# Attention and GEGLU block on one core: TensorE no longer waits for its own semaphore

## The chip, the cores and the metric

The kernel runs on one core of a Trainium2 chip. The metric is the device time of one execution in microseconds (us); before the change it is 1253.1 us, the median of 3 runs (1252.99 to 1253.51). Lower is better.

## What is computed

One transformer block on x of 2048 tokens x 512 features in bf16: a layer norm, attention with 32 heads of 16 features, a residual, a second layer norm, a GEGLU feed-forward of 1792 hidden features, a residual.

```python
qkv = (layernorm(x) @ wqkv) -> q, k, v          # 32 heads, Dh = 16
p = softmax(q @ k^T * Dh**-0.5)                 # 2048 x 2048 for each head
h = x + (p @ v) @ wo
out = h + (gelu(layernorm(h) @ w_gate) * (layernorm(h) @ w_up)) @ w_down
```

## The kernel before

**Units and ticks.** The queries are cut into 8 groups of 256 tokens, the heads into 8 slots of 4. A unit is one slot of one group: 64 units, 8 to a group. A unit has 16 ticks, and a group 128. In a tick two things happen to two units that lie 24 ticks apart:

- pass 1 (`p1_pair`, L797): two matmuls of 32 rows x 512 columns write scores into a pair of banks, and one VectorE reduce (`p1_consume`, L806) takes their row maxima. From tick 20 on the pairs are banks 0-1 and 2-3 in turn, so the pair of tick t is free again when the reduce of tick t-2 is done. 1024 ticks make 1024 reduces. At the end of a unit GpSimd joins the maxima, and a DMA transpose (L846) brings them back into the queries.
- pass 2 (`p2_tile`, L867): four matmuls of 32 rows x 256 columns write two banks, called tile a and tile b here, and two ScalarE exponentials (L879) take them to SBUF. These banks come from a pool of four, 4 to 7, one of which is lent to the dense stream at a time.

**The dense stream.** Behind pass 1 and pass 2 of a tick, TensorE gets one piece of a list of work items: the projections (L676, L739) early on; `item_pv`, probabilities times values (L893); `item_ofin` (L919); the output projection `item_oproj` (L998); `gate_up_mms` (L1072); `down_mm` (L1122). Where a tick has no piece, two dummy matmuls of 128 x 512 (L1285) stand there. An item of PV belongs to one unit and is cut into four pieces, each in a tick of its own. A piece is two halves of 8 matmuls (4 heads side by side in the array's columns, two key tiles one after the other), all 8 pieces of a unit's halves adding up in one bank. A feed-forward item and a projection item are cut into two pieces, a `down` item into pieces of three matmuls. The group's pieces go to TensorE in the order of the Python calls; all engines' orders are fixed when the program is built.

**Waits.** `Plan` keeps, for each tile and bank, its last writer and its readers since. `op` (L96) collects them as dependencies, `_waits_for` (L72) drops those that the engine is already known to have seen, and the rest become waits on the semaphores of the engines. A matmul with `sig=True` raises TensorE's semaphore when it completes; one with `sig=False` is given the token of the next one that signals (L107). A dependency on the own engine is dropped at L75 where its signal has not been issued yet (`v > e.count`), and where a wait for a reader implies it; otherwise TensorE waits for its own semaphore.

In PV the last matmul of each half signals (`sig=(g == 3 and i == 1)`, L893-895), and the first of the next half writes the same bank. In `gate_up_mms`, the projections and `down_mm` the earlier pieces do not signal, so their token is that of the next signal on TensorE: the second pass 1 matmul of the next tick. `group_begin` and `group_end` gather the waits of pass 1 and tile a at the first matmul of the tick.

Of the waits before the change, 580 instructions of TensorE wait for its own semaphore: 386 in PV (L893), 95 in gate and up (L1072), 57 in down (L1122), 27 in the projections (L676, L739), 14 in the output projection (L998), 1 in the warm-up (L427). In 569 of them it is the only wait and sits on the weight load of the matmul.

Of the kernel before, what the change touches and what calls it, by code (L numbers as in the profile page):

```python
# [15 lines left out]
class Plan:  # L16
# [55 lines left out]
    def _waits_for(self, e, deps, extra=()):  # L72
        need = {}
        for (k, v) in list(deps) + list(extra):
            if k == e.name and v > e.count:  # L75
                continue
            if v > need.get(k, 0):
                need[k] = v
        need = {k: v for k, v in need.items() if e.known.get(k, 0) < v}
        waits = []  # L80
        for k, v in sorted(need.items(), key=lambda kv: kv[0] == e.name):
            implied = {}
            for k2, v2 in need.items():
                if k2 != k and (k2, v2) not in self.dropped:
                    self._learn(implied, k2, v2)
            if implied.get(k, 0) >= v and self.behind.get((k, v)) is not None:
                self.dropped.add((k, v))
                continue
            waits.append((k, v))
        self.dropped.clear()  # L90
        for k, v in waits:
            self._learn(e.known, k, v)
        self.n_waits += len(waits)
        return waits
# [1312 lines left out]
```

## Time and profile before

| | |
|---|---|
| median of 3 runs | 1253.1 us |
| profiled execution, its own time | 1253.52 us |
| its span in the profile | 1251.8 us |
| TensorE matmul busy (PE) | 93 % |
| VectorE busy (DVE) | 95 % |
| ScalarE busy (ACT) | 96 % |
| GpSimd busy (POOL) | 61 % |

The span is the stretch that the profile shows; the execution's own time is 1.7 us longer. A "busy" share is the share of the span covered by instructions. Instructions that follow each other on an engine overlap: 23 reduces in a row, whose mean length is 1219 ns, take 26.03 us, 1.131 us each. PEld is TensorE's weight load, which runs beside its matmuls. A row of the timeline gives start, length, engine, line, operation, tiles and how many were merged, and in brackets how long the engine had been idle and what ended that.

### The profile page before, as it was taken

Reading aid. Unit: us, or ns where it says so; the run is one execution under the profiler, and the core shown is the slowest. Engines: PE = TensorE matmul, PEld = TensorE weight load, DVE = VectorE, ACT = ScalarE, POOL = GpSimd, SP = SyncE. Lnnn points to the kernel's source line nnn. Section 1 sums busy time; section 2 is a strip of 40 time slices with the busy share of each in tenths; the row PEclk is TensorE's granted clock in tenths of the full one; section 3 lists DMA queues with packets and bytes.
Section 4 is the critical chain, followed back from the end, with each engine's and each line's share of the span. In section 5 each row is a group of like instructions: output and inputs, shape, how many; then the busy total and the mean of one; then the engine's idle time right before and its main releaser. Section 6 shows DMA issues by size and latency. Waiting matters only on the chain.

```text
span 1251.8 us, 31448 instructions
## 1 busy us (share of the span) xinstructions
PE 1165.3 (93%) x12680; PEld 405.5 (32%) x12680; DVE 1193.7 (95%) x1088; ACT 1200.7 (96%) x2464; POOL 764.0 (61%) x1540
## 2 busy tenths in 40 slices
PE   8999998899999999999999999999999999999998
PEld 3222222233323333233323333233332333233335
DVE  8999999999999999999999999999999999999923
ACT  7899999999999999999999999999999999999992
POOL 7557774467746765376645776367654766547760
PEclk9999999999999999999999999999999999999989
DMA  4101004300010000200010000100001000100000
GB/s 150 31 21 28 24 19 129 88 6 3 6 31 12 6 6 6 38 5 6 4 26 18 3 6 6 26 17 6 6 4 39 6 4 6 26 19 3 6 13 18
DMA packets 50801, 27.45 MB, mean 22 GB/s; under 512 B 36065, under 2 KB 49633, under 8 KB 50657
## 3 DMA queue, kind: packets, MB, share of 16 engines
q1 hardware_dynamic: 50656, 25.45, 7.9%
q8 instruction: 101, 1.65, 0.5%
q14 instruction: 44, 0.35, 0.1%
HBM read 11.80 MB, written 2.10 MB: 11 GB/s over the span
## 4 chain that ended last, share of the span: by engine, by line
ACT 41%; PE 28%; DVE 27%; POOL 2%; issue 2%; DMA 0%; POOLq 0%
DVE PM L806 27%; ACT PTM L879 23%; ACT PTG L879 7%; PE pbank L893 7%; PE pbank L797 5%; PE pbank L867 4%; ACT PTE L879 4%; PE pbank L1122 4%; PE pbank L1285 3%; ACT th_sb L1055 2%; ACT g_sb L641 1%; PE pbank L1072 1%; PE pbank L739 1%; PE pbank L998 1%; ACT OA L641 1%
## 5 line engine op out<-in xcount | busy, mean ns | idle before, releaser
L806 DVE TENSOR_REDUCE PM<-pbank 128x2 f32<-128x1024 f32 x1024 | 1166.3, 1219 | 11.4 <-PE pbank L867 5.0
L879 ACT ACTIVATE PTM<-pbank 128x512 bf16<-128x512 f32 x1388 | 740.2, 672 | 11.2 <-PE pbank L867 4.5
L867 PE MATMUL pbank<-QT,KT 32*128 32x256 bf16 x4096 | 487.6, 273 | 5.4 <-ACT PTM L879 1.9
L797 PE MATMUL pbank<-KT,QT 32*128 32x512 bf16 x2048 | 394.1, 384 | 17.8 <-DVE PM L806 6.5
L1285 PE MATMUL pbank<-ones_bf,ident 128*128 128x512 bf16 x794 | 245.8, 385 | 23.6 <-ACT PTM L879 2.8
L879 ACT ACTIVATE PTG<-pbank 128x512 bf16<-128x512 f32 x420 | 228.4, 663 | 2.1 <-PE pbank L867 1.6
L797 PEld LDWEIGHTS pbank<-KT,QT 32*128 32x128 bf16 x2048 | 100.0, 91 | 356.2 <-DVE PM L806 164.7
L867 PEld LDWEIGHTS pbank<-QT,KT 32*128 32x128 bf16 x4096 | 159.5, 92 | 56.1 <-ACT PTM L879 30.5
L893 PE MATMUL pbank<-PTM,VA 128*17 128x256 bf16 x2776 | 154.8, 275 | 15.5 <-ACT PTM L879 0.6
L879 ACT ACTIVATE PTE<-pbank 128x512 bf16<-128x512 f32 x240 | 138.4, 672 | 2.6 <-PE pbank L867 1.5
L832 POOL TENSOR_TENSOR MX<-PM,MX 128x8 f32<-128x8 f32 x64 | 12.9, 202 | 162.9 <-DVE PM L806 162.9
L928 POOL TENSOR_TENSOR LINV<-OAT,negone 128x16 f32<-128x16 f32 (+1 forms) x32 | 92.7, 2896 | 0.0
L1285 PEld LDWEIGHTS pbank<-ones_bf,ident 128*128 128x128 bf16 x794 | 47.6, 97 | 126.0 <-ACT PTM L879 80.3
L893 PEld LDWEIGHTS pbank<-PTM,VA 128*17 128x17 bf16 x2776 | 42.7, 87 | 108.0 <-PE pbank L893 74.3
L821 POOL TENSOR_TENSOR MX<-PM,MX 128x8 f32<-128x8 f32 x64 | 13.0, 203 | 103.7 <-DVE PM L806 103.3
L1072 PE MATMUL pbank<-hnT_l,wu_sb 128*128 128x256 bf16 x448 | 66.7, 275 | 3.4 <-ACT PTM L879 0.2
L1072 PE MATMUL pbank<-hnT_l,wg_sb 128*128 128x256 bf16 x448 | 66.9, 275 | 2.5
L1114 POOL TENSOR_TENSOR GUT<-th_sb,u_sb 128x512 bf16<-128x512 f32 x49 | 62.3, 1271 | 4.5 <-DVE u_sb L630 2.4
L1061 POOL TENSOR_TENSOR th_sb<-th_sb,g_sb 128x512 f32<-128x512 f32 x49 | 62.1, 1268 | 4.1
L1062 POOL TENSOR_TENSOR th_sb<-g_sb 128x512 f32<-128x512 f32 x49 | 51.0, 1041 | 21.8 <-ACT g_sb L641 21.8
L1064 POOL TENSOR_TENSOR th_sb<-th_sb,g_sb 128x512 f32<-128x512 f32 x49 | 62.1, 1267 | 3.1
L1122 PE MATMUL pbank<-wd_sb,GUT 128*128 128x512 bf16 x224 | 60.7, 382 | 3.2 <-ACT PTM L879 0.2
(149 smaller groups left out, 1085.1 us busy)
## 6 DMA issues: line engine op xcount, KB each, us to landing
QKS<-QKS SPq DMA_DIRECT2D x27, 112.0 KB, 2.2
x_sb<-in_A_x_dram SPq DMA_DIRECT2D x4, 512.0 KB, 5.5
xres<-in_A_x_dram SPq DMA_DIRECT2D x16, 128.0 KB, 2.2
out_dram<-out_sb SPq DMA_DIRECT2D x16, 128.0 KB, 1.7
wg_sb<-in_B_w_gate_dram SPq DMA_DIRECT2D x4, 448.0 KB, 4.5
wu_sb<-in_B_w_up_dram SPq DMA_DIRECT2D x4, 448.0 KB, 4.0
wd_sb<-in_B_w_down_dram SPq DMA_DIRECT2D x3, 512.0 KB, 6.7
STG<-ST SPq DMA_TRANSPOSE x64, 2.3
```

What stands on the lines that cost most here:

```text
L797: P.op("pe", lambda e, g=g, b=b: e.matmul(pbank[:, b, :], QT[32 * g:32 * g + 32, c, slot, 128 * qt:128 * qt + 128], KT[32 * g:32 * g + 32, ...
L806: P.op("dve", lambda e: e.tensor_reduce(out=PM[:, par, qt, kc, g:g + 2], in_=pbank[:, b:b + 2, :], axis=AX.X, op=ALU.max), reads=[("pb", b ...
L867: P.op("pe", lambda e, kt=kt, i=i: e.matmul(pbank[:, b, 256 * i:256 * i + 256], KT[32 * g:32 * g + 32, slot, 128 * kt:128 * kt + 128], QT[ ...
L879: P.op("act", lambda e, b=b, pi=pi: e.activation(out=PTt(pi), in_=pbank[:, b, :], func=ACT.Exp), reads=[("pb", b)], writes=[("PT", pi)], e ...
L893: P.op("pe", lambda e, g=g, kt=kt, pi=pi, i=i: e.matmul(pbank[32 * g:32 * g + 17, b, 0:256], VA[:, kt, 4 * slot + g, :], PTt(pi)[:, 256 * ...
L928: P.op("pool", lambda e: e.tensor_tensor(out=li, in0=oat4[:, :, :, 16], in1=negone[:, 0:8 * ns].rearrange("p (q h) -> p q h", q=2), op=ALU ...
L1061: o(1.27, lambda e: e.tensor_tensor(out=ts_, in0=ts_, in1=gs, op=ALU.mult), [("th", par), ("g", par)])], then=done)
L1064: o(1.27, lambda e: e.tensor_tensor(out=ts_, in0=ts_, in1=gs, op=ALU.mult), [("th", par), ("g", par)])], then=lambda: defer(TANH_LAG, lamb ...
L1072: P.op("pe", lambda e, dc=dc, fc=fc, i=i: e.matmul(pbank[:, b, 256 * i:256 * i + 256], w[:, dc, 128 * fc:128 * fc + 128], hT[:, dc, :], st ...
L1114: P.op("pool", lambda e: e.tensor_tensor(out=o_ap, in0=shp(ts_), in1=shp(us), op=ALU.mult), reads=[("th", par), ("u", par)], writes=o_keys ...
L1122: P.op("pe", lambda e: e.matmul(pbank[:, b, :], GUT[:, fc, 128 * k:128 * k + 128], wd_sb[:, fc, :], start=first, stop=last), reads=[("GUT" ...
L1285: P.op("pe", lambda e: e.matmul(pbank[:, b, :], ident[:], ones_bf[:, 0:512], start=True, stop=True), reads=["ident", "ones_bf"], writes=[( ...
```

## The change

In `_waits_for` every dependency of TensorE on its own semaphore is dropped, not only the ones not yet signalled.

```diff
     def _waits_for(self, e, deps, extra=()):
         need = {}
         for (k, v) in list(deps) + list(extra):
-            if k == e.name and v > e.count:
+            if k == e.name and (v > e.count or k == "pe"):
                 continue
             if v > need.get(k, 0):
                 need[k] = v
```

All 580 waits go; 11 of these instructions keep waits for other engines. The order of the instructions on the five engines, the banks, the tiles, the signals and the waits of all other engines are the same.

## Prediction

> **What bounds the kernel now.** I read the page's engine rows first, then the waits, then the timeline tick by tick, and last the chain. DVE, ACT and PE are all over 90% busy, so the share of busy time does not name the bound.
>
> ```profile
> PE 1165.3 (93%) x12680; PEld 405.5 (32%) x12680; DVE 1193.7 (95%) x1088; ACT 1200.7 (96%) x2464; POOL 764.0 (61%) x1540
> ...
> ACT 41%; PE 28%; DVE 27%; POOL 2%; issue 2%; DMA 0%; POOLq 0%
> ...
> L806 DVE TENSOR_REDUCE PM<-pbank 128x2 f32<-128x1024 f32 x1024 | 1166.3, 1219 | 11.4 <-PE pbank L867 5.0
> ```
>
> The starts of the 1024 reduces decide it: 867 of the 1023 distances between them are 1.13 us, what a reduce needs when nothing holds it up. DVE is thus the pace of the whole middle, and only a tick that is late against 1.131 us costs time. Lateness over the whole span is 22.1 us: 5.7 in ticks 0 to 23, where the projections fill TensorE and, going by the order of waits, hardly any own wait stands, and **16.3 us after that**, in some 80 ticks. These 16.3 us and the end behind the last reduce are all that this change can touch. The waits of TensorE by releaser:
>
> ```profile
> PEld pbank L893 <- PE pbank L893: 104.7, 314, 0.4
> ...
> PEld pbank L1072 <- PE pbank L867: 13.4, 62, 0.3
> PEld pbank L1122 <- PE pbank L867: 12.4, 42, 0.3
> ```
>
> The first row is the second half of a PV piece waiting for the first. The reader is to see that 104.7 us of waiting is no gain of 104.7 us: most of it lies in ticks where DVE is not done either. A tick where it counts, from the timeline:
>
> ```profile
> 705.73 0.11 PEld L867 LDWEIGHTS pbank<-QT,KT 32*128 32x128 bf16 x2 [0.58 <-ACT PTE L879]
> ...
> 706.05 0.11 PEld L893 LDWEIGHTS pbank<-PTM,VA 128*17 128x17 bf16 x8 [0.21 <-issue]
> ...
> 706.52 0.11 PEld L893 LDWEIGHTS pbank<-PTM,VA 128*17 128x17 bf16 x8 [0.36 <-PE pbank L893]
> ...
> 706.85 0.39 PE L797 MATMUL pbank<-KT,QT 32*128 32x512 bf16 x2
> ...
> 707.28 3.49 DVE L806 TENSOR_REDUCE PM<-pbank 128x2 f32<-128x1024 f32 x3 [0.42 <-PE pbank L867]
> ```
>
> ACT let go of tile b's bank 0.7 us late (705.73). PV followed 0.32 us later, its second half 0.47 after the first, the next pass 1 0.33 after that, and the reduce 0.43 after pass 1: DVE stood idle for 0.42 us.
>
> **What each wait is worth on PE.** *PV, second halves: 256 of the 386.* From the first half's start to the second's is 0.469 us in every piece of the trace. A half is two rounds of 256 columns. Without the wait they should follow at the pitch of matmuls that wait for nothing: the chain has 48 matmuls of 256 columns in 5.24 us (L1072 in the tail), 0.109 each, so 0.22 for two. Saving 0.25 a piece. The bounds: 0.25, and nothing, if the array holds back a matmul that adds onto a region still being drained; within a half the second round already adds onto the first 0.11 us later, so I take 0.25. A PV tick falls from 0.33 + 0.47 + 0.33 = 1.13 us of PE, exactly DVE's pace, with no way to catch up, to 0.88. *PV, first halves: 130.* Their signal is a tick old: nothing. *down, 42 pieces.* Their first matmul starts 0.453 after pass 1, because the signal waited for is pass 1's own; the dummies, which wait for no such thing, start 0.332 after it (600.78 to 601.11). Saving 0.12: the tick falls from 1.206 to 1.086. *gate, up and projections, 122.* Also 0.45 against 0.33, but these ticks need only 0.99 us (0.45 + 0.54), and in the median the late tile b holds them until 0.65 anyway: nothing. *oproj, 14, and the warm-up's one*: hidden in the same way.
>
> **What of it reaches the end.** From about 300 us on the late ticks repeat in every group of 128 ticks (146.9 us). I follow each from the release before it that PE does not move.
>
> - *PV behind a late bank.* In the tick above ACT runs without a gap from 690.56 to 706.2, and it began when a tanh waited for GpSimd, which waited for a DMA and a reduce at 680.7. So 705.73 stays, and pass 1 comes 0.25 earlier. Six ticks of 0.51 late: 6 x 0.25 = 1.5. Ten more of 0.33 to 0.35: 10 x 0.25 = 2.5.
> - *PV ticks that were less than 0.25 late, or followed another PV*: seven of 0.20, five of 0.14, six of 0.05 and six single ones of 0.11 to 0.17 (62 to 83, 227 and 263 to 265 us) go to nothing: 1.4 + 0.7 + 0.3 + 0.8 = 3.2.
> - *down.* Six groups have four ticks that are 0.18, 0.08, 0.08 and 0.24 late. The 0.08 are the tick of 1.206. But ACT runs without a gap around them and gives tile b's bank 0.3 late in the first and the last, so the lateness mostly moves to the last. ACT itself begins its busy stretch some 0.24 earlier, since the PV ticks ahead of it (idle ACT 0.33 + 0.16 + 0.05) are shorter. Of 0.58 I take 0.24 as gone: 6 x 0.24 = 1.4, and 0.2 for ticks of 0.03 after the other down item.
> - *Not touched*: 1.2 us of late ticks with dummies behind a late bank (0.20 x 6), the projection ticks at 53 to 61 us, what is left above.
> - *Behind the last reduce* ACT is the pace until 1220.3; it idles ahead of exponentials at 1200.6, 1202.8 and 1218.8 for 0.12, 0.27 and 0.09 behind PV, and two PV halves after the last exponential save about 0.4: 0.9.
>
> The sum is 4.0 + 3.2 + 1.6 + 0.9 = **9.7 us**. Against the profiled execution's own 1253.52 that is 1243.8; that run was 0.4 above the median, so I predict **1243.4**.
>
> **The rivals.**
>
> *A, ACT, GpSimd and the DMA transposes decide, or the matmuls serialise anyway.* Then PV ticks keep their length, or the late banks move with them. For: ACT holds 41% of the chain, and the late ticks begin with an ACT release. Against: the reduce's idle time ends with PE, 0.43 after a pass 1 that PV held back, and ACT's distances between exponentials at their shortest, 0.478, leave it some 5% free. It would give 1251 to 1253.5.
>
> *B, nearly all lateness goes.* With PE at 0.88 in PV ticks ACT is fed earlier in every unit and its stretches start sooner, so the late banks go too. 16.3 + 0.9 would give 1236. Against: the tanh's wait on GpSimd starts ACT's stretch at 690.56 whatever PE does.
>
> *C, slower: the clock.* The granted clock was halved twice:
>
> ```profile
> 22.90:26.30 3.40, 3.40 (x12) 0.86 (x11) 2.87 (x4) 2.44 (x4) 3.21 (x6) 0.50 0.00 0
> 600.00:603.40 3.40, 3.35 (x32) 1.11 (x29) 3.40 (x4) 3.40 (x9) 0.54 (x4) 1.00 0.00 0
> ...
> 1207.35:1214.18 6.83, 6.32 (x28) 1.69 (x28) 0.30 (x1) 5.83 (x13) 6.58 (x7) 0.50 0.00 1
> ```
>
> The columns are the window, its length, busy time of PE, PEld, DVE, ACT and POOL, the clock, DMA share and GB/s. If idle PE drops the clock, PV ticks will do it now, since 0.25 of 1.13 us becomes idle. At half speed a PV tick's array time of 0.21 + 4 x 0.107 = 0.64 doubles, and with the 0.23 of switches the tick is 1.5, 0.37 more than DVE's pace; a drop of 3.4 us, the shortest seen, loses 0.37 x 2.3 = 0.85. Twelve drops eat the gain, fifteen make it slower by over 0.2%; one in each of 64 units would give 1243.4 + 54 = 1298. Against: a tick with dummies holds the same 0.64 of array time (0.21 + 2 x 0.21) and needs 0.87 of PE, and in the second row above, three such ticks, the clock stayed at 1.00. The Trainium skill speaks for this rival ("TensorE: Matmul & The Clock Gate", A second HAM failure mode: psum-queue depth-cycling): there, short idle times between groups of matmuls, in a kernel that cycles through PSUM banks, made the clock swing between half and full. The dummy ticks of this trace, which cycle through banks in the same way, do not show it.
>
> **How the numbers follow.** The forecast, 6 to 14 us faster, 0.72; B, 0.08; a smaller gain of 2.5 to 6 us, between the forecast and A, 0.08; A, 0.07; C, 0.05. A measurement of this kernel can tell about 0.2% (2.5 us) from no change. The smaller gain counts as faster, so faster is 0.88, same 0.07, slower 0.05. The range runs from just under B's 1236, 1235.5, to 1249.5, which cuts off half of the smaller gains, A and C: 0.16 left out.
>
> **What would show it.** The second half's weight load should start without the 0.36 of idle time, 0.22 after the first, and the row of 104.7 us should be gone, replaced by pass 1 waiting for DVE. Ticks of 0.20 and 0.14 late should be gone, those of 0.51 should be near 0.25 and those of 0.33 near 0.08. Wrong: second halves still at 0.47 (A); late ticks of 0.51 gone altogether (B); a clock under 1.00 between 30 and 1200 us (C).

## The result and the profile after

1243.37 us, the median of 4 runs (1242.92 to 1243.8), against 1253.17 us before: the ratio is 0.992, 95% interval 0.990 to 0.994. The change made the kernel 9.8 us faster. The profiled execution took 1243.15 us.

The page of the kernel after, the rows that answer to those of before:

```profile
PE 1137.8 (92%) x12680; PEld 437.8 (35%) x12680; DVE 1189.8 (96%) x1088; ACT 1199.9 (97%) x2464; POOL 764.3 (62%) x1540
...
DVE 58%; ACT 30%; PE 9%; POOL 2%; issue 1%; DMA 0%
...
L806 DVE TENSOR_REDUCE PM<-pbank 128x2 f32<-128x1024 f32 x1024 | 1162.4, 1224 | 5.3 <-PE pbank L867 2.8
```

TensorE's part of the chain that ended last fell from 28% to 9%, VectorE's rose from 27% to 58%: the reduce now sets more than half of it, ScalarE 30%. Of the reduce's idle time, 11.4 us, 5.3 are left. In the waits after, the row of 104.7 us (PV behind PV) is gone, and pass 1 waits for VectorE more often. The first row is from before, the two others from after:

```profile
PE pbank L797 <- DVE PM L806: 6.5, 35, 0.3
```

```profile
PEld pbank L893 <- issue: 40.3, 191, 0.2
...
PE pbank L797 <- DVE PM L806: 23.6, 103, 0.3
```

Where the time went, from the starts of the 1024 reduces in both traces:

| stretch of the span | before, us | after, us |
|---|---|---|
| up to the first reduce | 14.7 | 14.7 |
| lateness against 1.131 us a tick, ticks 0 to 23 | 5.7 | 4.7 |
| lateness, ticks 24 to 1022 | 16.4 | 7.3 |
| behind the start of the last reduce | 58.0 | 57.7 |

9.0 us are the change's work in the middle. The 0.3 at the end are no more than profiles differ there: that stretch is 57.7 and 57.6 us in two profiles of the kernel after, and 57.2 to 58.9 in those of the experiments. The 1.0 us at the start is not its doing: the clock was halved at 22.9 us in the profiled execution before, and not in the one after; of the profiles of the experiments below, with and without the waits, some have that drop and are 5.7 us late there, the others 4.7.

The tick shown before, in the kernel after (timeline, same group and tick):

```profile
699.83 0.11 PEld L867 LDWEIGHTS pbank<-QT,KT 32*128 32x128 bf16 x2 [0.64 <-ACT PTE L879]
...
700.15 0.33 PEld L893 LDWEIGHTS pbank<-PTM,VA 128*17 128x17 bf16 x16 [0.21 <-issue]
700.15 0.61 PE L893 MATMUL pbank<-PTM,VA 128*17 128x256 bf16 x16
...
700.70 0.39 PE L797 MATMUL pbank<-KT,QT 32*128 32x512 bf16 x2
```

The 16 weight loads of a piece are now one row: no idle time parts the halves. From PV's first matmul to the next pass 1 it is 0.55 us instead of 0.80; between the first matmuls of the halves 0.223 instead of 0.469 (their weight loads run ahead, 0.118 apart). And the tick is only 0.03 us late, not 0.51.

Late ticks by their place in a group of 128 (six groups, medians; five groups for tick 22):

| tick | what is behind pass 1 and 2 | late before, us | late after, us |
|---|---|---|---|
| 22 | PV | 0.14 | none |
| 48, 49, 50, 51 | down | 0.18, 0.08, 0.08, 0.24 | 0.17, none, none, 0.38 |
| 54 | PV | 0.05 | none |
| 56 | dummies | 0.20 | 0.26 |
| 86 | PV | 0.51 | 0.03 |
| 89 | PV | 0.33 | 0.08 |
| 119 | PV | 0.20 | none |

### The profile page after: what moved, and what is told of

The parts are those of the page before. It is cut to its first block, busy times and chain, and to the rows that moved or that the text cites. A ratio compares the mean times of both kernels' runs of the same rounds, so it can differ in the third digit from the quotient of the medians.

```text
span 1241.4 us, 31438 instructions
## 1 busy us (share of the span) xinstructions
PE 1137.8 (92%) x12680; PEld 437.8 (35%) x12680; DVE 1189.8 (96%) x1088; ACT 1199.9 (97%) x2464; POOL 764.3 (62%) x1540
## 4 chain that ended last, share of the span: by engine, by line
DVE 58%; ACT 30%; PE 9%; POOL 2%; issue 1%; DMA 0%
DVE PM L806 57%; ACT PTM L879 17%; ACT PTG L879 5%; ACT PTE L879 3%; PE pbank L1122 2%; PE pbank L867 2%; PE pbank L797 1%; ACT th_sb L1055 1%; PE pbank L1072 1%; ACT g_sb L641 1%; ACT OnT L1012 1%; ACT u_sb L641 1%; PE pbank L739 1%; PE pbank L998 1%; PE pbank L676 1%
## 5 line engine op out<-in xcount | busy, mean ns | idle before, releaser
L867 PE MATMUL pbank<-QT,KT 32*128 32x256 bf16 x4096 | 498.2, 273 | 9.7 <-ACT PTM L879 4.4
L797 PEld LDWEIGHTS pbank<-KT,QT 32*128 32x128 bf16 x2048 | 104.5, 91 | 392.7 <-DVE PM L806 170.3
L867 PEld LDWEIGHTS pbank<-QT,KT 32*128 32x128 bf16 x4096 | 164.5, 92 | 65.7 <-ACT PTM L879 36.8
L893 PE MATMUL pbank<-PTM,VA 128*17 128x256 bf16 x2776 | 125.8, 274 | 2.7 <-ACT PTM L879 1.2
L893 PEld LDWEIGHTS pbank<-PTM,VA 128*17 128x17 bf16 x2776 | 60.1, 89 | 46.9 <-issue 29.1
L1072 PE MATMUL pbank<-hnT_l,wu_sb 128*128 128x256 bf16 x448 | 67.1, 276 | 3.1 <-ACT PTM L879 0.2
L1072 PE MATMUL pbank<-hnT_l,wg_sb 128*128 128x256 bf16 x448 | 66.9, 275 | 2.5
```

The costliest lines, as they stand in the source:

```text
L797: P.op("pe", lambda e, g=g, b=b: e.matmul(pbank[:, b, :], QT[32 * g:32 * g + 32, c, slot, 128 * qt:128 * qt + 128], KT[32 * g:32 * g + 32, ...
L867: P.op("pe", lambda e, kt=kt, i=i: e.matmul(pbank[:, b, 256 * i:256 * i + 256], KT[32 * g:32 * g + 32, slot, 128 * kt:128 * kt + 128], QT[ ...
L893: P.op("pe", lambda e, g=g, kt=kt, pi=pi, i=i: e.matmul(pbank[32 * g:32 * g + 17, b, 0:256], VA[:, kt, 4 * slot + g, :], PTt(pi)[:, 256 * ...
L1072: P.op("pe", lambda e, dc=dc, fc=fc, i=i: e.matmul(pbank[:, b, 256 * i:256 * i + 256], w[:, dc, 128 * fc:128 * fc + 128], hT[:, dc, :], st ...
```

## The experiments

**Theory.** The 256 waits of the second halves of PV cost all of it. Without them TensorE has a lead over VectorE again after each late bank, and ScalarE gets its scores earlier. **Rivals:** each of the 580 waits costs something, met or not; the down ticks carry a good part; what is left late is TensorE's or a DMA's.

### The waits of second halves alone, and all others alone

`own` is a new argument of `op`; where it is false, a dependency of TensorE on itself is dropped.

```diff
-writes=[("pb", b)], sig=(g == 3 and i == 1))
+writes=[("pb", b)], sig=(g == 3 and i == 1), own=(m % 2 == 0))
```

> Own waits dropped at the 256 second halves of the PV pieces alone; the other 324 (130 first halves, 95 gate and up, 57 down, 27 projections, 14 output projection, 1 warm-up) stay. Theory (only the second halves stand between a late bank and pass 1): 1243.4 to 1244.2 us, nearly all of the gain; down ticks again 0.075 late in the middle of their four, the four together about as late as without the waits (0.55 to 0.58). Rival (each own wait costs something, met or not): 256 of 580 waits give 256/580 of 9.8 us, 1248.8 us.

Measured: 1244.13 us (1243.64 to 1245.84, 5 runs), ratio 0.993 (0.992 to 0.995). The theory held, the rival of 1248.8 did not. Lateness after tick 24 is 9.0 us; ticks 49 and 50 are 0.076 late again and tick 51 is 0.24; with tick 48's 0.15 that is 0.54 us. In three of the six groups of the profiled run tick 74 is 0.12 to 0.32 late and tick 86 0.26; in the other three neither is late. In just these three groups the DMA transpose of the maxima was late at the same place: from GpSimd's last step before it to the use of its result 4.28, 4.37 and 4.46 us, against 3.76 in the others, and GpSimd idled behind it for 0.47 to 0.66.

In the counterpart only the second halves wait:

```diff
-extra_deps=(), own=True):
+extra_deps=(), own=False):
...
+writes=[("pb", b)], sig=(g == 3 and i == 1), own=(m % 2 == 1))
```

> The other part alone: the 256 waits of the second halves stay, the other 324 are dropped. Theory: 1252.5 to 1253.2 us, late ticks of 0.51, 0.33 and 0.20 as before. Rival (each own wait costs something): 1247.7 us. If down ticks were worth what the prediction gave them (1.6 us): 1251.5 us.

Measured: 1251.72 us (1251.12 to 1252.18), ratio 0.999 (0.998 to 1.000). That is a gain of 1.2 us, under the theory's 1252.5, and far from 1247.7. By its time alone it could be the 1251.5 that the down ticks would give; the ticks say otherwise. The ticks of 0.51, 0.33 and 0.20 stand at 0.50, 0.33 and 0.20. In the four down ticks the two of 0.08 are gone and the last is 0.38 instead of 0.24: the time moved, as 0.149 + 0.378 = 0.53 shows. What is gained is small change: 0.02 to 0.04 in ticks 22, 34 and 48 of each group, some 0.55 us in all, one tick of 0.17, and 0.4 behind the last reduce, which is within the differences there.

### Odd units and even units

Nearly all the late PV ticks belong to odd units. The kernel for the even units has `ui % 2 == 1` in this place.

```diff
-sig=(g == 3 and i == 1))
+sig=(g == 3 and i == 1), own=(m % 2 == 0 or ui % 2 == 0))
```

> Own waits dropped at the 128 second halves of PV pieces of odd units (those that run in the ticks that were late), the rest as before. If a late bank's release stays where it is and PV behind it only shortens (the prediction's step): ticks of 0.51 become 0.25, those of 0.33 become 0.08, of 0.20 and 0.14 go; 7 to 8 us gained, 1245.2 to 1246.2 us. Theory from the profile after (PV of even units feeds ScalarE earlier, so the release itself moves by 0.23 as well): the same here, since even units keep their waits, but then 0.03 instead of 0.25 needs both.

Measured: 1247.24 us (1246.77 to 1248.44), ratio 0.996 (0.995 to 0.997). The tick in question, in the timeline:

```profile
703.18 0.11 PEld L867 LDWEIGHTS pbank<-QT,KT 32*128 32x128 bf16 x2 [0.83 <-ACT PTE L879]
703.50 0.33 PEld L893 LDWEIGHTS pbank<-PTM,VA 128*17 128x17 bf16 x16 [0.21 <-issue]
704.05 0.39 PE L797 MATMUL pbank<-KT,QT 32*128 32x512 bf16 x2
...
704.48 1.23 DVE L806 TENSOR_REDUCE PM<-pbank 128x2 f32<-128x1024 f32 x1 [0.17 <-PE pbank L867]
```

PV behind the bank is as short as in the kernel after, and the tick is 0.25 late in all six groups, just what the prediction gave it. Tick 89 is 0.08 late, tick 119 0.11 and not gone, and a tick of 0.06 is new in each group. That makes 1 us less than expected.

> Own waits dropped at the 128 second halves of PV pieces of even units, in which hardly a tick was late. If the release of a late bank stays (the prediction's step): almost nothing, 1252.3 to 1253 us, ticks of 0.51 unchanged. Theory (TensorE's lead over VectorE grows in these ticks, ScalarE is fed earlier and begins its stretch without a gap earlier): six ticks of 0.51 become about 0.28, 1.4 us, and with two early ticks and the end 1251.0 to 1251.6 us.

Measured: 1250.57 us (1249.93 to 1251.63), ratio 0.998 (0.997 to 0.999), 0.4 us under what the theory gave.

```profile
703.63 0.11 PEld L867 LDWEIGHTS pbank<-QT,KT 32*128 32x128 bf16 x2 [0.58 <-ACT PTE L879]
703.95 0.11 PEld L893 LDWEIGHTS pbank<-PTM,VA 128*17 128x17 bf16 x8 [0.21 <-issue]
704.41 0.11 PEld L893 LDWEIGHTS pbank<-PTM,VA 128*17 128x17 bf16 x8 [0.36 <-PE pbank L893]
704.75 0.39 PE L797 MATMUL pbank<-KT,QT 32*128 32x512 bf16 x2
...
705.17 1.23 DVE L806 TENSOR_REDUCE PM<-pbank 128x2 f32<-128x1024 f32 x1 [0.37 <-PE pbank L867]
```

PV behind the bank is as long as before, with its 0.36 of idle time, and still the tick is 0.27 late instead of 0.51 (five of six groups; 0.45 in the other, where the transpose of the maxima took 4.09 us instead of 3.76). So the bank itself came 0.24 earlier against VectorE: PV of the even unit one block of 16 ticks ahead had let ScalarE start earlier. The two halves of the cause add up: 0.25 + 0.24 of 0.51. Tick 119 falls from 0.20 to 0.11 in the one run and 0.12 in the other, and goes with both.

### The clock: fewer dummies

The second kernel of the two has 1 in the place of 0.

```diff
             if p1_ok:
-                want = 2
+                want = 0 if p2_started else 2
```

> The changed kernel without the dummy matmuls from tick 24 to the last tick of pass 1 (426 of 794 rows of them fewer; the output is not concerned). It tests rival C of the prediction, that idle time on TensorE halves its clock. If it does: the clock falls under 1.00 between 30 and 1200 us; a tick with a PV piece at half speed needs about 1.5 us, each drop of 3.4 us costs up to 0.85 us, dozens of drops give 1255 to 1300 us. If it does not: the clock stays at 1.00, the ticks of 0.26 with a dummy behind a late bank shorten, 1241.5 to 1243.4 us.

Measured: 1311.39 us (1302.43 to 1321.3), ratio 1.047 (1.043 to 1.051). The row of the granted clock in 40 slices, and two stretches of it (window, its length, busy time of PE, PEld, DVE, ACT, POOL, clock, DMA share, GB/s):

```profile
PEclk9997777687898776877888877788889878787879
```

```profile
423.40:440.40 17.00, 15.76 (x152) 5.92 (x152) 14.82 (x14) 15.30 (x32) 9.99 (x20) 0.50 0.01 1
440.60:454.00 13.40, 9.75 (x150) 4.43 (x146) 13.33 (x13) 13.19 (x28) 11.71 (x17) 1.00 0.03 6
```

At 1.00 the reduces run without a gap (13.33 of 13.40 us), and TensorE is busy for 9.75; at 0.50 TensorE is busy for 15.76 of 17.00 us, and VectorE waits. Between 30 and 1190 us the clock was halved for 406 us in all, and lateness after tick 24 rose from 7.3 to 74.2 us. The commonest lateness is 0.38 (78 ticks), as the prediction's 0.37. The rival that the prediction called C is a real mechanism; the kernel after did not meet it in either of its two profiles.

> The changed kernel with one dummy matmul instead of two in each of those ticks, half the idle time of the run without dummies. If the clock falls below some share of busy time: between the changed kernel and the run without dummies, with fewer drops, or none. If it does not fall at all: 1242 to 1243.6 us.

Measured: 1248.25 us (1246.06 to 1250.43), ratio 0.996 (0.995 to 0.998), some 5 us slower than the kernel after. In its profile the clock was halved six times between 30 and 1190 us, for 3.4 or 6.8 us; tick 56 is 0.04 late instead of 0.26, so the dummies themselves do cost there. TensorE's busy share goes with the drops: 92% in the kernel after (no drop between 30 and 1190 us), 87% here, 84% without dummies.

### What is still late: ScalarE

Square of the second layer norm on 64 columns instead of 512, so that 7/8 of each sum of squares is left out:

```diff
-e.activation(out=hn_sb[:, k, :], in_=hh, func=ACT.Square, ...)
+e.activation(out=hn_sb[:, k, 0:64], in_=hh[:, 0:64], func=ACT.Square, ...)
```

> The changed kernel with ScalarE's Square of the second layer norm (L1012, 512 columns, twice a group) cut to its first 64 columns, so that the variance is wrong: it leaves out 7/8 of that work, some 0.37 us each. Theory (what is left of the late ticks, 0.38 and 0.26 in each of six groups, is ScalarE's overload around the output projection): both shrink by about the time taken away, to under 0.1, 1239.5 to 1241 us. Rival (they come from TensorE's down pieces or from DMA): unchanged, 1243 to 1243.8 us.

Measured: 1240.17 us (1238.86 to 1240.32), ratio 0.990 (0.989 to 0.991). Groups by line, shapes, count, busy time, mean ns; in the kernel after and here:

```profile
L1012 ACT ACTIVATE OnT<-xres 128x512 bf16<-128x512 bf16 x14 | 9.8, 697 | 0.0
```

```profile
L1012 ACT ACTIVATE OnT<-xres 128x64 bf16<-128x64 bf16 x14 | 4.4, 314 | 0.0
```

0.38 us less of ScalarE, twice a group, and the ticks of 0.38 (51) and 0.26 (56) are gone in all six groups; tick 48, ahead of the Squares, keeps 0.14. TensorE's down pieces were not touched. (Two groups of this run have a late transpose, 4.34 and 4.44 us, and again ticks 74 and 86 late, the latter by 0.26.) What ticks 51 and 56 lose is ScalarE's burst.

The same work, later:

```diff
-            defer(2, sq)
+            defer(14, sq)
```

> The changed kernel with the two Squares of a group issued about ten ticks later (defer of 14 ticks instead of 2), after ScalarE's stretch without a gap; nothing is left out. If lateness is ScalarE's burst there: 0.38 and 0.26 shrink or go, 1239.5 to 1242 us, unless the later feed-forward puts its own bursts where there is no slack. If ScalarE's load only moves with it: 1243 to 1245 us.

Measured: 1242.06 us (1241.85 to 1245.32), ratio 0.992 (0.991 to 0.993), the same as the kernel after within the interval. Ticks 51 and 56 are no longer late, but tick 84 is 0.33, 90 0.09 and 121 0.08: the burst moved. In the profiled run one tick was 1.0 late: TensorE stood idle for 1.31 us ahead of a gate matmul (L1072 at 833.15), and the clock fell for 3.4 us behind it.

### Attempts to go on

```diff
-                want = 2
+                want = 0 if p2_started and tick % 128 == 56 else 2
```

> The changed kernel without the two dummy matmuls of one tick in each group, tick 56 of 128, the one that is 0.26 late with dummies behind a late bank. If what is left there is the dummies' own time behind ScalarE's release: 0.26 becomes 0.04 as with one dummy everywhere, six times 0.22, 1241.9 to 1242.6 us, and the clock stays at 1.00, since one tick in 128 is no idle window. If ScalarE alone sets it: unchanged, 1243 to 1243.8 us.

Measured: 1242.54 us (1241.6 to 1243.53), ratio 0.992 (0.991 to 0.993). Tick 56 is no longer late, the clock stays at 1.00 between 30 and 1190 us, and the median is 1.2 us under that of the kernel after on the same chip (below), with intervals that overlap.

> The version with the two Squares of a group issued later, without the dummies of tick 84 of 128, which is 0.33 late there. Expected: 0.33 goes, six times 0.3, 1240 to 1241 us, the fastest so far. If the lateness moves to the next PV ticks: 1241.5 to 1242.2 us.

The edit is that of the later Squares with the dummies left out at tick 84. Measured: 1248.84 us (1245.98 to 1252.08), ratio 0.997 (0.996 to 0.998): a miss. Lateness moved to ticks 85 and 86 (0.19 + 0.17), and the clock fell. In the profile the first drop of the middle follows a stretch in which TensorE had half of its time idle:

```profile
831.70:835.10 3.40, 1.70 (x20) 0.82 (x20) 2.59 (x4) 1.90 (x5) 0.65 (x4) 1.00 0.05 6
835.10:838.50 3.40, 3.40 (x24) 1.24 (x21) 3.00 (x3) 3.11 (x7) 1.94 (x4) 0.50 0.00 0
```

TensorE stood there for the first gate matmul of the group, whose input is transposed by a DMA (L988) issued at 829.9 us; the matmul started at 833.9. With the Squares later this transpose is just in time, and in that group it was not; the profile of the later Squares alone has the same gap there. The second drop, of 3.4 us at 992.1, has another place: it follows a tick 84, whose reduce starts at 990.4 and whose dummies are left out, and in the 3.4 us ahead of it TensorE was never idle for more than 0.23 us at a time. The clock also speaks for the dummies: its mean is 0.989 to 0.995 over the six runs here, and 0.996 to 1.000 over the five of the later Squares alone (on another chip), from which this kernel differs only by the dummies of tick 84. So most likely leaving them out lowered the clock, which leaving out those of tick 56 did not. Why the one tick can do without them and the other cannot is open.

The kernel after once more, on the chip of the two runs above:

> The changed kernel as it is, on the same chip as the two others. 1243.0 to 1243.8 us. In its profile, like in those before: lateness of 9 us less after tick 24 than in the kernel before, and the first 24 ticks 4.7 or 5.7 us late according to whether the clock was halved at 23 us, which is the same for both kernels.

Measured: 1243.76 us (1243.53 to 1244.04), ratio 0.993 (0.992 to 0.994): 9.0 us faster than the kernel before on that chip (1252.78). Lateness after tick 24 is 7.2 us, and 4.7 in the first 24 ticks.

## Why the prediction was right, and where it was not

The time, 1243.4, was met to within 0.1 us. That closeness is partly luck. Two steps were off by 1.4 us in opposite directions, and the end gave 0.6 less than its term: by the two profiles the change's work is 9.0 us in the middle and 0.3 at the end, against the 9.7 of the sum.

- *VectorE's 1.131 us is the pace, and only 16.3 us and the end can be touched.* Right. The distances between reduces that are at the pace (within 0.009 us) rose from 867 to 927 of 1023, and 9.0 of 16.4 us went.
- *Second halves of PV: 0.25 us each on TensorE.* Right: 0.469 became 0.223, a PV tick 1.13 became 0.88. The bound of nothing did not come: the second half starts 0.223 behind the first, two rounds at the 0.109 of matmuls that wait for nothing, though it adds onto what the first has just written. The row of 104.7 us counts 314 waits, so 58 of them stand at first halves, and not all at second ones.
- *First halves, gate, up, projections, output projection: nothing.* Right to about 1 us: all waits but the second halves' are worth 1.2 us (0.999, 0.998 to 1.000), 0.4 of it behind the last reduce.
- *"So 705.73 stays, and pass 1 comes 0.25 earlier."* **This step failed** for the ticks of 0.51: 0.03 was left, not 0.25, 1.4 us more gain than put in the sum. The release moved by 0.23 to 0.24 against VectorE. The group that I followed was not typical: its DMA transpose took 4.30 us to the use of its result, 3.76 in the five others (GpSimd idle for 0.50 us behind it), and so in that group alone the tanh waited for GpSimd. One group later, at 837.44 us of the trace before, the same tanh waits for nothing; ScalarE's stretch without a gap begins behind PV of an even unit, where three of its exponentials start 0.12, 0.33 and 0.16 us later than the shortest distance of 0.48, for TensorE. The odd and even runs part the two halves of it. For groups with a late transpose the working was right: five of them, in the profiles of two experiments, keep 0.26. The two rows below are GpSimd's use of the transpose (L851) before, in the group followed and in the next.

```profile
686.80 0.67 POOL L851 TENSOR_TENSOR QT<-QT,STG 128x256 bf16<-128x256 bf16 x1 [0.50 <-DMA STG<-ST]
...
833.33 0.67 POOL L851 TENSOR_TENSOR QT<-QT,STG 128x256 bf16<-128x256 bf16 x1
```

- *Ticks of 0.33: 0.08 left.* Right. *Ticks of 0.20 and 0.14 gone.* Right, though those of 0.20 needed PV of both kinds of units; of the six single ones two stayed (0.14 and 0.16). *Ticks of 0.05 gone*: they moved two ticks on, where 0.20 became 0.26.
- *down: 0.24 of 0.58 goes in each group.* **Wrong**: ticks 48 to 56 together were 0.82 late and are 0.82 late. The 0.08 twice did go, as worked out (tick 1.206 became 1.09), but the lateness moved whole to ticks 51 and 56, because ScalarE sets it (Square cut: gone). I had ScalarE begin that stretch 0.24 earlier, behind the shorter PV ticks at 651 to 653 us. But it waits for TensorE once more, just ahead of tick 44 of the group, where two exponentials start 0.51 apart before and 0.72 after, which uses up what it had gained. Pass 1 of tick 44 starts 0.90 ahead of its reduce before and 0.88 after: with or without the waits it cannot run further ahead, as its pair of banks comes free with the reduce two ticks back. Of the 1.6 us of this term only the 0.2 at tick 34 came.
- *Behind the last reduce: 0.9 us.* 0.3 measured, within the differences between profiles; what the prediction had wrong there is open.
- *Rivals.* A did not happen. B was half right in its reason (ScalarE is fed earlier) and wrong in its size. C did not happen in this kernel, and two runs show how near it is. The Trainium skill's rule on it ("TensorE: Matmul & The Clock Gate", A second HAM failure mode: psum-queue depth-cycling), that idle times between groups of matmuls make the clock swing, agrees with these two runs: 0.50 and 1.00 in turn, and in the 3.4 us ahead of each drop TensorE's longest idle time was 0.15 to 0.76 us.

## What to carry to other kernels

A wait of TensorE for its own earlier matmul, where only the order of writes to a bank matters, parts two runs of matmuls that could follow each other: 0.25 us each here, and it is paid in the ticks whose slack is already used up, so count late ticks against the pace of the bounding engine, not the total of the wait. Before an idle time is called fixed because another engine released it, look at what fed that engine, in more than one repetition of the pattern: one late transfer made the group followed here the exception. And when TensorE gets faster, watch its clock: the filling that looks useless may be what keeps it up (1311 us without it, 1243 with it).

## What was not expected of the hardware

- The clock fell without TensorE ever being idle for long: without dummies, with 84% of the span busy by the page, it was halved for 406 of the 1160 us in the middle, and with one dummy (87%) for 24 us. The share alone does not tell: at 92% it was not halved there in the kernel after, but for 3.4 us with the Squares later and for 6.8 us with tick 84's dummies left out as well. Nearly every stretch was a multiple of 3.4 us.
- The DMA transpose of the maxima (L846) scatters from run to run and group to group. At the place followed it is 3.76 us from GpSimd's last step before it to the use of its result, which is what GpSimd's other work takes in between, or 4.3 to 4.5 where the transpose came later than that: in six of eighteen groups of three profiles (before, second halves alone, Square cut), and in none of the eight other profiles with the Squares in their old place, where 4.20 is the most. In the trace before SyncE issued nothing else within 5 us of the late one. Each of the five late ones in the two experiments cost its group 0.35 to 0.55 us in ticks 74 and 86.
